# A Fourier mixer beside a gated feed-forward on one core: halved matmul groups at both ends, one product's order and one call's weights

## The chip, the cores and the metric

The kernel runs on one core of a Trainium2 chip. The metric is the device time of one launch in microseconds (us). Engines are called as the profile calls them: PE does the matmuls and PEld its weight loads, ACT and DVE work on rows of up to 128 partitions, POOL is nearly unused, and SP issues most DMAs. PSUM is the memory that PE writes, in banks of 512 fp32 columns; SBUF holds everything else on the chip.

## The reference

Input x has 2048 rows of 576 columns. After a layernorm over the columns two branches read it, and the result is the sum of x and both:

```
xn = layernorm(x)
A  = irfft2(rfft2(xn) * (w_r + i w_i))            # over rows and columns
B  = (sigmoid(xn @ w_gate) * (xn @ w_up)) @ w_down  # 576 -> 4608 -> 576
out = x + A + B
```

All of it is fp32. The kernel splits each operand of a product into a high part and a low part in PE's own format and adds three products (high x high, high x low, low x high).

## The kernel before, in words

**The feed-forward.** The 2048 rows are two pairs of 1024 rows; the columns F are 36 blocks of 128. One *unit* is one block of F for one pair: seven products of Strassen's scheme, each seven matmuls of 128x512 (`unit`, L709; `prod`, L643; `STEPS` lists the parts). The weights of a block arrive raw, ACT copies the high part (L257) and DVE subtracts the low part (L259, L261) and forms the sums that the seven products need (L281 to L284); `make_w` does this in nine pieces, and `turn(n)` advances it by n pieces at given places between the products. The down product is done per tile of 128 rows (`down`, L771): twelve matmuls of 128x288 into two PSUM banks, one for each half of the 576 columns, then one DVE add to the accumulator `acc` (L789), and for the very last block the DMA to `out` (L796): rows 0 to 63 on SP's queue, rows 64 to 127 on ACT's. The tiles still to do stand in `pend`.

**The opening.** Before the seven products can start, the first two blocks of the first pair are done plainly as four *calls* (u, c), c being the half of the 1024 rows: (0,0), (1,0), (0,1), (1,1). `opening` (L947) writes out the order by hand: moments and scales of two tiles of rows (`scaled`), `normalise` (L410, on ACT: x * rstd + nmr), transposes of the normalised tile on PE (`lift`, L430; identity weights, into PSUM), the high part on ACT (L437) and the low part on DVE (L438) into X, the transposed operand. X has five planes: two high, one remainder of 32 columns, two low. While PE has nothing to do, `identity(n)` (L929) has it multiply an identity n times. After that come the gate product and the up product of call (0,0) in `plain_late` (L691): for gate and up, and for k = 1, 2, first the six steps of `LOW_LAST` (high and low planes), then, when the remainders have been transposed (`mid`, L443 and L445), the last step. Inside `opening` most instructions go through `strictly`, which keeps program order on their engine; from the third call on `strict` is off, and the framework's scheduler orders each engine's instructions by what it expects to be ready.

**The loop over calls.** Calls three and four, (0,1) and (1,1), run `beside(i)` after each of their four products (i = 0 to 3): a down tile if there is one, then `turn(3)`. In the fourth call `make` is `make_w(2)`, the weights of the first proper unit. The same turns advance the sums and transposes for the seven products (`factors`: L418 to L425, L397, L402, L434, L443), which are in `sides`.

**The Fourier branch.** It is cut into three phases that run beside the second pair's units (`phase1b`, `phase2`, `phase3`), a piece per step (`aside`). In `phase3` (L548, 16 tiles) the inverse over the columns is this: the middle 2 x 128 frequencies and a left-over of 34 are transposed into `pz`, ACT and DVE split the former (z3h, z3l), ACT then copies the latter (z3r, L591), and a piece later come, for even and odd frequencies, one matmul of the left-over with 288 columns (L595) and six of 144 columns (L599), then ACT's copy `od` (L601).

Tile tags name PSUM: "pp" is a pair of banks with two buffers (`pair`), "bA", "bB" single banks, "bE" a bank with two buffers.

Of the kernel before, what the change touches and what calls it, by code (L numbers as in the profile page):

```python
# [13 lines left out]
OP = mybir.AluOpType  # L14
# [144 lines left out]
def spectral_glu_kernel(ctx: ExitStack, tc: tile.TileContext, x, xt, xg, ri, w_in, w_down, out):  # L159
# [11 lines left out]
    def pair(name):  # L171
        return ps.tile([P, 2, 512], F32, tag="pp", name=name, bufs=2)
# [71 lines left out]
    def strictly(ins):  # L244
        if strict[0]:
            tc.keep_in_program_order(ins)
# [163 lines left out]
    def normalise(m, c):  # L410

        t = c * TPC + m
        b, src = XS[m][:, 2 * c:2 * c + 2], acc[t].rearrange("p (a d) -> p a d", a=2)
        strictly(nc.scalar.activation(b, src, AF.Identity, bias=nmr[:, t:t + 1], scale=rstd[:, t:t + 1]))

    def sums_12(m):
        A11, A12, A21, A22, S1 = (XS[m][:, i] for i in range(5))
# [130 lines left out]
    def phase3(t):  # L548
# [43 lines left out]
        yield  # L592
        pe = pair(f"pe{t}")
        for e in range(2):
            nc.tensor.matmul(pe[:, e, :HD], zr[:3 * FR, e, :], dr[:3 * FR, e, :], start=True, stop=False, skip_group_check=True)  # L595
            for k in range(2):
                o = pe[:, e, (k + 1 + e) % 2 * HQ:((k + 1 + e) % 2 + 1) * HQ]
                for n, (l, i) in enumerate(((zh, 0), (zl, 0), (zh, 1))):
                    nc.tensor.matmul(o, l[:, k, e, :], di[:, e, k, i, :], start=False, stop=n == 2, skip_group_check=True)  # L599
        od = pool.tile([P, HD], F32, tag="od", name=f"od{t}")  # L600
        nc.scalar.activation(od, pe[:, 1, :HD], AF.Copy)  # L601
        V = pool.tile([P, 2, 2, HQ], F32, tag="ev", name=f"ev{t}")
# [37 lines left out]

    LOW_LAST = ((0, 0), (1, 1), (0, 3), (1, 4), (3, 0), (4, 1))

    def prod(bank, w, x, start, stop, skip=False, steps=STEPS):  # L643
        for j, (sx, sw) in enumerate(steps):
            strictly(nc.tensor.matmul(bank, w[:, sw, :], X[:, x, sx, :], start=start and j == 0,  # L645
                                    stop=stop and j == len(steps) - 1, skip_group_check=skip))

    def end():
# [5 lines left out]
        H[u] = (hh, hl)  # L654
        return hh, hl

    def new_plain(u, c):

        g = hp.tile([P, 2, CW], F32, tag="gv"[u % 2], name=f"g{u}_{c}", bufs=1)
        bank = [ps.tile([P, CW], F32, tag=f"b{b}", name=f"p{b}{u}_{c}", bufs=2 if b == "E" else 1) for b in ("AB"[u % 2], "E")  # L660
                if (u, c, b) != (0, 1, "A")]
        if len(bank) == 1:
            bank.insert(0, pair("pg")[:, 0])
        return g[:, 0], bank

    def gate(G_, bank):
# [9 lines left out]
    def of_plain(u, c, b, k):  # L676
        return WS[u][:, WP[f"B{k}{b + 1}"]], XA[f"A{c + 1}{k}"]
# [10 lines left out]
            beside(i)  # L688
        plain_ends(u, c, G_, bank)

    def plain_late(u, c, beside, mid):  # L691

        G_, bank = new_plain(u, c)
        beside(-1)
        for i, (b, k) in enumerate(((0, 1), (0, 2), (1, 1), (1, 2))):
            prod(bank[b], *of_plain(u, c, b, k), k == 1, False, steps=LOW_LAST)
            end()
            mid(i)
            if i < 3:
                beside(i)  # L700
        for b in range(2):
            for k in (1, 2):
                prod(bank[b], *of_plain(u, c, b, k), False, k == 2, steps=STEPS[-1:])
            if b == 0 and (u, c) != (0, 0):
                gate(G_, bank)
        beside(3)
        return G_, bank
# [63 lines left out]
    def down(p, j, m):  # L771

        t = p * TPP + m
        c, cols = m // TPC, slice((m % TPC) * P, (m % TPC + 1) * P)
        pd = pair(f"po{j}_{t}")
        for g in range(G):
            u = p * NF + j * G + g
            if (u, c) in HS:
                h, w = HS[u, c], [WF[j, g, b] for b in range(2)]
                h, w = [h[:, i, cols] for i in range(2)], [[w[b][:, i] for b in range(2)] for i in range(2)]  # L780
            else:
                h, w = [v[:, c, cols] for v in H[u]], [[WD[u][:, i, b * HD:(b + 1) * HD] for b in range(2)] for i in range(2)]
            for n, (i, k) in enumerate(((0, 0), (0, 1), (1, 0))):
                for b in range(2):
                    nc.tensor.matmul(pd[:, b, :HD], h[i], w[k][b], start=g == 0 and n == 0, stop=g == G - 1 and n == 2)  # L785

        def add():
            a = acc[t].rearrange("p (b d) -> p b d", b=2)
            nc.vector.tensor_tensor(a, a, pd[:, :, :HD], op=OP.add)  # L789
# [152 lines left out]
    def both(c, mm, mains):  # L942
        return zip(*(lift(f"A{c + 1}{h + 1}", mm, main) for h, main in enumerate(mains)))
# [3 lines left out]
    def opening():  # L947
# [48 lines left out]
        first = plain_late(0, 0, lambda i: None, mid)  # L996
        load_raw(2)
        keep_p(0)

# [213 lines left out]
    for p in range(PAIRS):  # L1213

        calls = [(0, 0), (1, 0), (0, 1), (1, 1)] if p == 0 else [(0, 0), (0, 1), (1, 0), (1, 1)]
        for n, (f, c) in enumerate(calls):
            u = p * NF + f
            if p == 0 and n == 2:
                sides += [make_d(0, 2), make_d(1, 2)]
            elif p and c == 0:  # L1220
                wd = get_d(u)
            if p == 0 and n < 2:
                if n == 0:
                    opening()
# [24 lines left out]
            if n == 3:  # L1249
                finish(make)  # L1250
# [86 lines left out]
```

## Time and profile before

| | before |
|---|---|
| median of 3 runs | 1414.44 us (1414.28 to 1415.12) |
| the profiled execution's own time | 1414.13 us |
| its span (first to last instruction) | 1412.3 us |
| PE busy | 1398.7 us, 99% of the span |
| DVE busy | 1116.6 us, 79% |
| ACT busy | 642.4 us, 45% |
| DMA | 341.48 MB, mean 242 GB/s |

How to read it: a row of the timeline gives the start in us from the span's start, the busy time, engine, line, operation, out<-in by the program's names, shape and count; neighbours of one kind are merged into one row. In brackets stands the engine's idle time before it and what ended that. A matmul's own duration overlaps the next one's, so the price of one in a stream is the distance between two starts, not its duration. The busy share is an average over stages with different limits, and has to be read stage by stage.

### The profile page before, as it was taken

Reading aid. Unit: us, or ns where it says so; the run is one execution under the profiler, and the core shown is the slowest. Engines: PE = TensorE matmul, PEld = TensorE weight load, DVE = VectorE, ACT = ScalarE, POOL = GpSimd, SP = SyncE. Lnnn points to the kernel's source line nnn. Section 1 sums busy time; section 2 is a strip of 40 time slices with the busy share of each in tenths; the row PEclk is TensorE's granted clock in tenths of the full one; section 3 lists DMA queues with packets and bytes.
Section 4 is the critical chain, followed back from the end, with each engine's and each line's share of the span. In section 5 each row is a group of like instructions: output and inputs, shape, how many; then the busy total and the mean of one; then the engine's idle time right before and its main releaser. Section 6 shows DMA issues by size and latency. Waiting matters only on the chain. (4 is left out here: it accounts for less than half of the span.)

```text
span 1412.3 us, 20690 instructions
## 1 busy us (share of the span) xinstructions
PE 1398.7 (99%) x7883; PEld 1230.3 (87%) x7883; DVE 1116.6 (79%) x1723; ACT 642.4 (45%) x1032; POOL 3.3 (0%) x5
## 2 busy tenths in 40 slices
PE   8999999999999999999999999999999999999998
PEld 6888888888888888888888888888888889888887
DVE  6998888888888888789466888867878878777884
ACT  6654444444444444443245554435545534443431
POOL 0000000000000000000000000000000000000000
PEclk9999999999999999999999999999999999999999
DMA  6588677777777776665777777678888787776643
GB/s 251 219 311 322 254 271 262 271 262 271 261 269 262 268 263 236 249 250 181 268 224 222 222 229 232 202 246 267 277 265 272 239 280 217 246 223 202 194 127 84
DMA packets 128738, 341.48 MB, mean 242 GB/s; under 512 B 11936, under 2 KB 49344, under 8 KB 123904
## 3 DMA queue, kind: packets, MB, share of 16 engines
q1 hardware_dynamic: 127712, 338.86, 70.9%
q8 instruction: 62, 1.02, 0.3%
q10 hardware_dynamic: 928, 1.31, 0.3%
q14 instruction: 36, 0.29, 0.1%
HBM read 203.99 MB, written 136.13 MB: 241 GB/s over the span
## 5 line engine op out<-in xcount | busy, mean ns | idle before, releaser
L645 PE MATMUL pB<-X,w 128*128 128x512 f32 x1484 | 380.4, 394 | 0.9 <-ACT pB L729 0.5
L645 PEld LDWEIGHTS pB<-X,w 128*128 128x128 f32 x1484 | 267.7, 188 | 51.5 <-ACT v L742 1.4
L645 PE MATMUL pE<-X,w 128*128 128x512 f32 x1064 | 272.4, 392 | 0.1
L645 PE MATMUL pA<-X,w 128*128 128x512 f32 x994 | 255.5, 392 | 0.3 <-ACT X L437 0.3
L645 PEld LDWEIGHTS pE<-X,w 128*128 128x128 f32 x1064 | 193.1, 188 | 35.6 <-DVE y L743 0.7
L785 PE MATMUL po<-wd,hh 128*128 128x288 f32 x1216 | 210.9, 295 | 0.0
L645 PEld LDWEIGHTS pA<-X,w 128*128 128x128 f32 x994 | 180.1, 188 | 32.7 <-ACT X L437 0.5
L876 PEld LDWEIGHTS ps<-wf,hs 128*128 128x128 f32 x1260 | 188.6, 188 | 20.7 <-DVE acc L886 2.0
L876 PE MATMUL ps<-wf,hs 128*128 128x288 f32 x1260 | 202.5, 296 | 0.7 <-DVE acc L886 0.4
L785 PEld LDWEIGHTS po<-wd,hh 128*128 128x128 f32 x1216 | 184.1, 188 | 11.8 <-ACT hh L768 0.4
L789 DVE TENSOR_TENSOR acc<-acc,po 128x576 f32<-128x576 f32 x168 | 125.9, 750 | 61.6 <-PE po L785 61.1
L257 ACT ACTIVATE w<-raw 128x768 fp32r<-128x768 f32 (+1 forms) x106 | 100.8, 952 | 94.8 <-PE pE L645 39.9
L785 PE MATMUL po<-wd,hl 128*128 128x288 f32 x608 | 128.7, 293 | 0.0
L886 DVE TENSOR_TENSOR qs<-qs,ps 128x576 f32<-128x576 f32 x112 | 84.1, 751 | 24.9 <-PE ps L876 24.0
L785 PEld LDWEIGHTS po<-wd,hl 128*128 128x128 f32 x608 | 98.7, 189 | 0.0
L743 DVE TENSOR_TENSOR y<-v,pE 128x512 f32<-128x512 f32 x68 | 46.7, 687 | 50.6 <-ACT v L742 49.8
L763 DVE TENSOR_TENSOR y<-y,g 128x1024 f32<-128x1024 f32 x67 | 81.9, 1223 | 3.2
L886 DVE TENSOR_TENSOR acc<-acc,ps 128x576 f32<-128x576 f32 x90 | 67.5, 751 | 21.1 <-PE ps L876 20.4
L259 DVE TENSOR_TENSOR w<-raw,w 128x512 fp32r<-128x512 f32 (+1 forms) x106 | 81.9, 773 | 2.4 <-ACT w L257 2.1
L812 ACT ACTIVATE hs<-y 128x512 fp32r<-128x512 f32 x105 | 65.0, 631 | 41.3 <-DVE y L763 14.8
L746 ACT ACTIVATE g<-pB 128x512 f32<-128x512 f32 x68 | 40.7, 599 | 88.9 <-PE pB L645 88.8
L813 DVE TENSOR_TENSOR hs<-y,hs 128x512 fp32r<-128x512 f32 x105 | 71.2, 687 | 3.9 <-ACT hs L812 3.0
(171 smaller groups left out, 1572.4 us busy)
## 6 DMA issues: line engine op xcount, KB each, us to landing
w<-wsp SPq DMA_DIRECT2D x246, 320.0 KB, 3.5
wsp<-w SPq DMA_DIRECT2D x34, 2240.0 KB, 7.8
raw<-in_w SPq DMA_DIRECT2D x34, 768.0 KB, 9.7
wdsp<-wd SPq DMA_DIRECT2D x36, 576.0 KB, 4.7
wf<-tsp SPq DMA_DIRECT2D x60, 288.0 KB, 3.5
wf<-wdsp SPq DMA_DIRECT2D x45, 288.0 KB, 3.9
std<-in_wd SPq DMA_DIRECT2D x36, 288.0 KB, 5.4
ri<-in_ri SPq DMA_DIRECT2D x16, 580.0 KB, 5.4
```

What stands on the lines that cost most here:

```text
L257: placed(nc.scalar.activation(o[:, :, :3, :], src, AF.Copy))
L259: placed(nc.vector.tensor_tensor(o[:, :, 3:, :], src[:, :, :KT, :], f32(o[:, :, :KT, :]), op=OP.subtract))
L645: strictly(nc.tensor.matmul(bank, w[:, sw, :], X[:, x, sx, :], start=start and j == 0, stop=stop and j == len(steps) - 1, skip_group_check ...
L743: nc.vector.tensor_tensor(y[:, 1], v[:, 1], bank["E"], op=OP.add)
L746: nc.scalar.activation(g[:, 1], bank["B"], AF.Sigmoid)
L763: nc.vector.tensor_tensor(y, y, g, op=OP.mult)
L785: nc.tensor.matmul(pd[:, b, :HD], h[i], w[k][b], start=g == 0 and n == 0, stop=g == G - 1 and n == 2)
L789: nc.vector.tensor_tensor(a, a, pd[:, :, :HD], op=OP.add)
L812: nc.scalar.activation(hs[:, 0], src, AF.Copy)
L813: return lambda: nc.vector.tensor_tensor(hs[:, 1], src, f32(hs[:, 0]), op=OP.subtract)
L876: nc.tensor.matmul(pd[:, i, :HD], h[:, a, m], w[:, b], start=q == 0, stop=q == 2)
L886: nc.vector.tensor_tensor(o, o, pd[:, :, :HD], op=OP.add)
```

## The change

Four edits.

1. *First gate product in column halves.* The gate product of call (0,0) is done on columns 0 to 255 of its bank as soon as the first two row tiles are in X, and on columns 256 to 511 in `plain_late` as before. The parts of the first half stand where fillers stood: two steps for each k, then three fillers where there were ten, then the transposes of tiles 2 and 3, then the four other steps. The last step (remainder) stays at full width. The bank "bA" is taken in `opening`; the transposes use the two "bE" banks first and a bank of each "pp" pair second. The normalise of tile 3 goes from ACT to DVE.
2. *Inverse over d.* In `phase3` the left-over's matmul comes behind the six others of its half, not ahead of them.
3. *Last down tile.* For the very last tile the twelve matmuls are sorted by column half, into banks "bA" and "bB"; each half has its own add, and its own store: columns 0 to 287 on SP's queue, 288 to 575 on ACT's, all 128 rows.
4. *Weights of one call later.* In the calls of the first pair the turn behind the first product (i = 0) advances `make` by no piece instead of three. Only the fourth call has something to make there.

```diff
-        strictly(nc.scalar.activation(b, src, AF.Identity, bias=nmr[:, t:t + 1], scale=rstd[:, t:t + 1]))
+        if t == 3:
+            strictly(nc.vector.tensor_scalar(b, src, rstd[:, t:t + 1], nmr[:, t:t + 1], op0=OP.mult, op1=OP.add))
+        else:
+            strictly(nc.scalar.activation(b, src, AF.Identity, bias=nmr[:, t:t + 1], scale=rstd[:, t:t + 1]))
...
         for e in range(2):
-            nc.tensor.matmul(pe[:, e, :HD], zr[:3 * FR, e, :], dr[:3 * FR, e, :], start=True, stop=False, skip_group_check=True)
             for k in range(2):
                 o = pe[:, e, (k + 1 + e) % 2 * HQ:((k + 1 + e) % 2 + 1) * HQ]
                 for n, (l, i) in enumerate(((zh, 0), (zl, 0), (zh, 1))):
-                    nc.tensor.matmul(o, l[:, k, e, :], di[:, e, k, i, :], start=False, stop=n == 2, skip_group_check=True)
+                    nc.tensor.matmul(o, l[:, k, e, :], di[:, e, k, i, :], start=k + n == 0, stop=False, skip_group_check=True)
+            nc.tensor.matmul(pe[:, e, :HD], zr[:3 * FR, e, :], dr[:3 * FR, e, :], start=False, stop=True, skip_group_check=True)
...
-    def prod(bank, w, x, start, stop, skip=False, steps=STEPS):
+    def prod(bank, w, x, start, stop, skip=False, steps=STEPS, cols=slice(0, CW)):
         for j, (sx, sw) in enumerate(steps):
-            strictly(nc.tensor.matmul(bank, w[:, sw, :], X[:, x, sx, :], start=start and j == 0,
+            strictly(nc.tensor.matmul(bank[:, cols], w[:, sw, :], X[:, x, sx, cols], start=start and j == 0,
...
+            if begun and b == 0:
+                prod(bank[b], *of_plain(u, c, b, k), False, False, True, LOW_LAST, HALF[1])
+            else:
+                prod(bank[b], *of_plain(u, c, b, k), k == 1, False, steps=LOW_LAST)
...
-        pd = pair(f"po{j}_{t}")
+        if together:
+            po = pair(f"po{j}_{t}")
+            pd = [po[:, b, :HD] for b in range(2)]
+        else:
+            pd = [ps.tile([P, CW], F32, tag=f"b{b}", name=f"po{j}_{t}_{b}", bufs=1)[:, :HD] for b in "AB"]
...
+        for b, l, r, start, stop in todo if together else sorted(todo, key=lambda v: v[0]):
+            nc.tensor.matmul(pd[b], l, r, start=start, stop=stop)
...
+            if not together:
+                for b in range(2):
+                    nc.vector.tensor_tensor(a[:, b], a[:, b], pd[b], op=OP.add)
+                    (nc.sync, nc.scalar)[b].dma_start(out[t, :, b * HD:(b + 1) * HD], a[:, b])
+                return
...
-        p1 = pair("px_A11")
-        p2 = [ps.tile([P, CW], F32, tag="bE", name=f"px_A12_{i}", bufs=2) for i in range(2)]
-        his, lows = both(0, 0, (p1[:, 0], p2[0]))
+        p1 = [ps.tile([P, CW], F32, tag="bE", name=f"px_{i}", bufs=2) for i in range(2)]
+        his, lows = both(0, 0, p1)
         for f in his:
             f()
-        identity(10)
+        bA = ps.tile([P, CW], F32, tag="bA", name="pA0_0", bufs=1)
+
+        def left(steps, first=False):
+            for k in (1, 2):
+                prod(bA, *of_plain(0, 0, 0, k), first and k == 1, False, True, steps, HALF[0])
+
         level(0, 1)
+        left(LOW_LAST[:2], True)
+        identity(3)
+        his2, lows2 = both(0, 1, [pair(f"px_A1{i + 1}")[:, 0] for i in range(2)])
         next(W[0, 2])
         for f in lows:
             f()
-        his, lows = both(0, 1, (p1[:, 1], p2[1]))
+        his, lows = his2, lows2
+        left(LOW_LAST[2:4])
+        left(LOW_LAST[4:])
         for f in his + lows:
             f()
...
-                    turn(3 if p == 0 else 1)
+                    turn(1 if p else 3 * (i > 0))
...
-        down(*pend.pop(0))()
+        down(*pend.pop(0), together=bool(pend))()
```

More of the change, by code (lines that the diff above doesn't have):

```diff
@@ L655, in new_h, with new_plain @@
         return hh, hl
-    def new_plain(u, c):
+    HALF = slice(0, CW // 2), slice(CW // 2, CW)
+    def new_plain(u, c, begun=None):
         g = hp.tile([P, 2, CW], F32, tag="gv"[u % 2], name=f"g{u}_{c}", bufs=1)
         bank = [ps.tile([P, CW], F32, tag=f"b{b}", name=f"p{b}{u}_{c}", bufs=2 if b == "E" else 1) for b in ("AB"[u % 2], "E")
-                if (u, c, b) != (0, 1, "A")]
+                if (u, c, b) not in ((0, 0, "A"), (0, 1, "A"))]
         if len(bank) == 1:
-            bank.insert(0, pair("pg")[:, 0])
+            bank.insert(0, begun or pair("pg")[:, 0])
         return g[:, 0], bank
@@ L702, in plain_late @@
             for k in (1, 2):
[L703 removed]
+                prod(bank[b], *of_plain(u, c, b, k), False, k == 2, bool(begun) and b == 0, steps=STEPS[-1:])
             if b == 0 and (u, c) != (0, 0):
@@ L784, in down @@
                 for b in range(2):
-                    nc.tensor.matmul(pd[:, b, :HD], h[i], w[k][b], start=g == 0 and n == 0, stop=g == G - 1 and n == 2)
+                    todo.append((b, h[i], w[k][b], g == 0 and n == 0, g == G - 1 and n == 2))
+        for b, l, r, start, stop in todo if together else sorted(todo, key=lambda v: v[0]):
+            nc.tensor.matmul(pd[b], l, r, start=start, stop=stop)
         def add():
             a = acc[t].rearrange("p (b d) -> p b d", b=2)
-            nc.vector.tensor_tensor(a, a, pd[:, :, :HD], op=OP.add)
+            if not together:
[3 more added lines that the diff above has]
+                return
+            nc.vector.tensor_tensor(a, a, po[:, :, :HD], op=OP.add)
             if j == NF // G - 1:
@@ L994, in mid @@
                     f()
-        first = plain_late(0, 0, lambda i: None, mid)
+        first = plain_late(0, 0, lambda i: None, mid, bA)
         load_raw(2)
```

8 lines of the change are left out of this document (4 added, 4 removed).

## The prediction

> **What bounds the kernel now.** I read the page first, for the engine that is never idle.
>
> ```profile
> span 1412.3 us, 20690 instructions
> PE 1398.7 (99%) x7883; PEld 1230.3 (87%) x7883; DVE 1116.6 (79%) x1723; ACT 642.4 (45%) x1032; POOL 3.3 (0%) x5
> ```
>
> PE is busy for 1398.7 of 1412.3 us, so an edit pays only if it takes work off PE, closes one of the few gaps in it, or shortens what lies after its last matmul. The table of windows says where the gaps can be (columns: stretch, then busy us and count of PE, PEld, DVE, ACT, POOL, then the granted clock and the DMA share).
>
> ```profile
> 40.00:50.00 10.00, 9.65 (x64) 8.69 (x62) 9.65 (x21) 7.29 (x15) 0.00 (x0) 1.00 0.50 179
> 50.00:60.00 10.00, 9.88 (x58) 8.56 (x59) 9.89 (x19) 6.32 (x13) 0.00 (x0) 1.00 0.76 289
> 60.00:100.00 40.00, 39.47 (x210) 33.41 (x208) 37.09 (x58) 21.92 (x34) 0.00 (x0) 1.00 0.78 292
> 100.00:300.00 200.00, 200.00 (x1110) 177.21 (x1109) 164.40 (x238) 91.50 (x120) 0.00 (x0) 1.00 0.77 280
> ```
>
> From 100 us on PE has no gap worth the name; a gain won earlier is carried to the end. From 40 to 60 us DVE is as full as PE (9.65 and 9.89 of 10): there the order of DVE's work decides who waits. The rest lies in the opening and behind the last matmul.
>
> **First gate product in halves, and the normalise moved to DVE.** The opening on PE, from the timeline (start, busy time, instruction):
>
> ```profile
> 10.21 2.54 PE L931 MATMUL b<-idr 128*128 128x512 f32 x10
> 12.58 1.05 PE L434 MATMUL px_A<-idf,xa 128*128 128x128 f32 x8
> 13.89 3.06 PE L645 MATMUL pA<-X,w 128*128 128x512 f32 x12 [0.25 <-ACT X L437]
> 16.78 1.52 PE L645 MATMUL pE<-X,w 128*128 128x512 f32 x6
> 18.15 0.70 PE L443 MATMUL px_r<-idr,rm 128*96 128x128 f32 x8
> 24.21 1.03 PE L434 MATMUL px_A<-idf,xa 128*128 128x128 f32 x8
> 28.00 0.44 PE L434 MATMUL px_A<-idf,xa 128*128 128x128 f32 x2 [0.24 <-ACT xa L414]
> ```
>
> The ten fillers (identity) stand from 10.21 to 12.58, 0.237 us each; the change keeps three, so 7 x 0.237 = 1.66 us of idle work goes. The twelve gate matmuls (13.89 to 16.78, 0.241 each) become 24 of 256 columns, twelve of them in the fillers' place. No 256-column matmul stands in the trace. Bounds are the nearest widths, 144 and 288:
>
> ```profile
> 1169.05 0.39 PE L599 MATMUL pe<-dit,z3h 128*128 128x144 f32 x2
> 1169.27 0.28 PE L599 MATMUL pe<-dit,z3l 128*128 128x144 f32 x1
> 1398.05 9.78 PE L785 MATMUL po<-wb,hp 128*128 128x288 f32 x72 [0.32 <-DVE acc L789]
> ```
>
> The two matmuls of 144 columns that start at 1169.05 take until the next starts at 1169.27, 0.11 each; 72 of 288 take 9.78 us, 0.136 each. I take 0.125, nearer the 288-wide row: 24 x 0.125 = 3.0 against 2.89 us, a loss of 0.1 (bounds: a gain of 0.25, a loss of 0.4). PE is left with 1.55 us less to do before 16.78. How much of it is seen depends on ACT and DVE:
>
> ```profile
> 10.05 1.09 ACT L437 ACTIVATE X<-px_A 128x512 fp32r<-128x512 f32 x2 [0.36 <-PE px_A L434]
> 11.03 1.63 ACT L414 ACTIVATE xa<-acc,nmr,rstd 128x576 f32<-128x576 f32 x2
> 13.24 1.09 ACT L437 ACTIVATE X<-px_A 128x512 fp32r<-128x512 f32 x2 [0.59 <-PE px_A L434]
> 10.60 0.68 DVE L259 TENSOR_TENSOR w<-raw,w 128x512 fp32r<-128x512 f32 x1
> 11.74 1.29 DVE L438 TENSOR_TENSOR X<-px_A,X 128x512 fp32r<-128x512 f32 x2
> 13.87 1.29 DVE L438 TENSOR_TENSOR X<-px_A,X 128x512 fp32r<-128x512 f32 x2 [0.84 <-ACT X L437]
> 16.27 0.63 DVE L402 TENSOR_TENSOR rm<-xa,rm 128x64 fp32r<-128x64 f32 x4
> 16.82 0.81 DVE L364 BATCH_NORM_STATS2 st<-acc 128x6 f32<-128x288 f32 x2
> ```
>
> Walk it. The first half products need the high parts (ACT L437, 10.65 and 11.14): they run until about 11.4, three fillers until 12.15. That wait is new; behind it on PE stand the fillers and the transposes, which could not have started before 11.9 anyway. The second transposes need both normalised tiles; ACT alone had them at 12.66, now its one is done at 11.9 and DVE's sooner, so they start near 12.2, 0.35 us earlier, and end at 13.1. Eight more halves until 14.1, the twelve of the second half until 15.6: the up product starts at 15.6 and not 16.78, 1.2 us earlier.
>
> DVE must keep up. The normalise goes in front of its L259 at 10.60. It is not on DVE in this trace; I bound it by one 288-column pass (two L364 take 0.81, so 0.41) and by DVE's 576-column add (0.75, the L789 rows below), and take 0.55. The low parts then end at 13.65 instead of 13.03, and the second pair, which before waited 0.84 us for ACT, at about 15.0 against 15.16: the added pass fits into that wait. The four L402 are then done at 16.6 to 17.0, and PE wants them (L443) at 18.15 - 1.2 = 16.95: just in time, 0.05 lost.
>
> Here a page can be weighed. The Trainium skill, VectorE: DVE Perf Modes, "Mode 2×_2P", says that a one-source fp32 operation from SBUF to SBUF streams two elements a cycle. No row here shows that; by it the pass would be near the lower bound and the 0.05 would vanish, without it near the upper and some 0.1 would be lost. Neither end changes the sum by more than 0.1.
>
> Does the lead survive the next stretch? At 24.21 PE transposes, then:
>
> ```profile
> 25.28 0.60 ACT L437 ACTIVATE X<-px_A 128x512 fp32r<-128x512 f32 x1 [2.49 <-PE px_A L434]
> ```
>
> ACT idles 2.49 us for PE; behind this copy on ACT stands the square root of the next two tiles' scales, whose normalise PE waits for at 28.00. That chain hangs on PE's own arrival, so it moves with it. **Value: -1.15 us**; bounds -0.4 (the halves at 0.136 and DVE late for L443) and -1.45 (all PE work saved).
>
> **Left-over product last in the inverse.** The same 14 matmuls in another order, 16 times.
>
> ```profile
>   ACT z3r L591: 0.5, 2
> ```
>
> This row is from the left-over product's own view (L595, idle time before it and how often): its weight load waited for ACT twice, 0.5 us in all. So that wait is 0.5 us at most. The order itself: a 288-wide matmul at the end hides the next weight load better than a 144-wide one, an estimate of a few hundredths each time from the 0.11 and 0.136 above. **Value: -0.3**; bounds -0.8 and +0.5 (0.03 us lost each time). ACT's copy (od) waits for the end of the group, which does not move.
>
> **Last down tile in halves.** The last add, the last two stores in the DMA view (KB, us from issue to landing), and an add of 288 columns from another place:
>
> ```profile
> 1407.87 0.75 DVE L789 TENSOR_TENSOR acc<-acc,po 128x576 f32<-128x576 f32 x1 [0.83 <-PE po L785]
> out<-acc SPq DMA_DIRECT2D x1, 144.0 KB, 2.4
> out<-acc ACTq DMA_DIRECT2D x1, 144.0 KB, 2.7
> L604 DVE TENSOR_TENSOR ev<-pe,od 128x288 f32<-128x288 f32 x32 | 13.1, 452 | 11.1 <-ACT od L601 11.1
> ```
>
> Sorted by half, the first six matmuls end 6 x 0.136 = 0.8 us before the last, at 1407.05; their add falls into DVE's idle 0.83 us, and its DMA leaves while PE works. Behind the last matmul stands one add of 288 columns (L604, 0.45) instead of 0.75: -0.3. Both stores wait for the one add, leave together, and the second landed 0.3 us after the first, 2.7 against 2.4; with the first gone some 0.8 us ahead, the last should land like one by itself, -0.35 or more. Its rows are 1152 bytes and twice as many, which can eat some of that. **Value: -0.7**; bounds -0.3 (the add alone) and -1.1.
>
> **Weights of one call later.** In the fourth plain call the first of four turns no longer advances the splitting of the next weights. Moved by one turn, in DVE's order: L259, L261 and L281; behind them the second and third turn's work, the store of the split weights and the load that reuses their buffer (both on SP's queue; the reloaded buffer is split one unit later, so nothing near waits for it). What the present order costs:
>
> ```profile
> 49.16 0.69 DVE L259 TENSOR_TENSOR w<-raw,w 128x512 fp32r<-128x512 f32 x1
> 49.34 0.30 PE L443 MATMUL px_S<-idr,rma 128*96 128x128 f32 x1
> 49.76 0.22 DVE L402 TENSOR_TENSOR rma<-xa,rma 128x64 fp32r<-128x64 f32 x1
> 50.12 0.24 PE L443 MATMUL px_S<-idr,rma 128*96 128x128 f32 x1 [0.48 <-ACT w L257]
> ```
>
> PE's two transposes stand 0.78 us apart because the second needs L402, which stood behind the weights' L259. With the weights later L402 goes first, and most of that gap closes. **Value: -0.5**; bounds -0.7 (this whole gap) and +6.3, the rival below. What is late next: the weights themselves.
>
> **Sum.** 1.15 + 0.3 + 0.7 + 0.5 = 2.65 us. The profiled execution took 1414.13 us, 1.8 over its span; the median of the three runs is 1414.44, 0.3 above it. So 1414.4 - 2.65 = **1411.8 us**, for the median.
>
> **Rivals.**
>
> 1. *The DVE-laden stretch pays more.* The scheduler orders everything after the opening anew, and from 60 to 100 us PE idles another 0.53 us while DVE is 93% busy. If that goes too and the tail and the inverse reach their better bounds (0.4 and 0.5 more), the sum is 4.1: 1410.3 us. For it: all these gaps end on DVE or ACT. Against it: they are small and scattered.
> 2. *The opening's lead is swallowed.* If DVE's added pass is at its upper bound and L402 makes PE wait, or the scheduler gives the lead back between 40 and 60 us where DVE is full, the opening yields 0.4 and the weights nothing: 1.4 in all, 1413.0 us. Against it: DVE waited 0.84 us for ACT just there.
> 3. *The clock.* Three fillers instead of ten leave short gaps while the clock is young. The first fillers show what a slow clock costs:
>
> ```profile
> 3.79 5.79 PE L931 MATMUL b<-idr 128*128 128x512 f32 x15 [3.79 <-DMA idr<-c_id]
> ```
>
> 15 in 5.79 us, 0.386 each, against 0.237 later. If 24 halves ran at that rate, 24 x 0.125 x 0.63 = 1.9 us would be lost: 1413.7. The Trainium skill, TensorE: Matmul & The Clock Gate, "What's actually happening", says that an idle window of about 3.4 us throttles the array; no gap in my walk is over 0.5 us, so by that rule this doesn't happen.
> 4. *Slower: the weights come too late.* DVE has 0.1 us to spare between 50 and 60 us. One turn is the distance between the weights' first two copies:
>
> ```profile
> 43.02 1.17 ACT L257 ACTIVATE w<-raw 128x1152 fp32r<-128x1152 f32 x1
> 47.10 0.85 ACT L257 ACTIVATE w<-raw 128x768 fp32r<-128x768 f32 x1 [0.84 <-DVE raw L281]
> 49.27 0.85 ACT L257 ACTIVATE w<-raw 128x768 fp32r<-128x768 f32 x1 [0.74 <-DVE raw L284]
> 51.20 0.41 DVE L261 TENSOR_TENSOR w<-raw,w 32x256 fp32r<-32x256 f32 x1
> 55.69 1.76 PE L645 MATMUL pE<-X,w 128*128 128x512 f32 x7
> ```
>
> 4.1 and 2.2 us. The last split ended at 51.61; the second product of the next unit starts at 55.69. So it decides at a delay of 4.1 us: one turn just fits, and one DVE task more does not. If this unit and the one after each wait their turn (4.1 and 2.2), 6.3 us are lost against 2.15 won elsewhere: 1418.6 us. Against it: that product needs only the second of three parts, and PE has down tiles to put in between.
>
> That an edit does nothing is nearest for the inverse, which removes 0.5 us of waits at best; it is in the range.
>
> **How the numbers follow.** Forecast 0.50, its own range 1410.8 to 1412.8; rival 1 0.25, rival 2 0.10, rival 3 0.05, rival 4 0.10. A measurement of this kernel can tell about 0.2%, 2.8 us, from no change: under 1411.6 is faster, over 1417.2 slower. The forecast stands at that edge and is split, 0.28 faster and 0.22 the same. Faster 0.28 + 0.25 = 0.53; the same 0.22 + 0.10 + 0.05 = 0.37; slower 0.10. The range takes in the forecast and rivals 1 to 3; at the low side 1 us under rival 1 for the better bounds of the opening and the weights (0.3 and 0.2) and for the scattered gaps, at the high side up to no gain at all. It leaves out rival 4: 1409.3 to 1414.4.
>
> **What would show it.** Right: the up product (pE) starting near 15.6; the second transposes near 12.2; 24 pA matmuls at 0.12 to 0.13; the transposes of 24.21 near 23.1; the two L443 at 49 us without a gap; a last add of 0.45 us and about 4.1 us from its start to the span's end; PE's waits for z3r gone. Wrong: a PE wait for DVE L402 near 17; PE waits on w in 52 to 70 us; halves at 0.2 us; a stretch after 100 us that grows.

## The result, and the profile after

| | before | after |
|---|---|---|
| median of 22 runs each, on one chip | 1414.75 us (1414.15 to 1415.59) | 1412.49 us (1411.56 to 1413.15) |
| ratio | | 0.9984, 95% interval 0.9978 to 0.9989 |
| the profiled execution's own time | 1414.13 us | 1413.03 us |
| its span | 1412.3 us | 1411.2 us |

The changed kernel is 2.26 us faster (1.6 to 3.1 by the interval). That is 0.16%, inside the bound of 0.2% that the prediction called the same. Its span fell by only 1.1 us: this one profile lost time at two places by late transfers, as told below.

The page's line of engines, then three of the windows that were shown of before (stretch, then busy us and count of PE, PEld, DVE, ACT, POOL, granted clock, DMA share, GB/s):

```profile
PE 1397.6 (99%) x7888; PEld 1229.3 (87%) x7888; DVE 1116.8 (79%) x1725; ACT 640.5 (45%) x1031; POOL 3.3 (0%) x5
```

```profile
40.00:50.00 10.00, 10.00 (x67) 9.22 (x66) 9.80 (x21) 7.08 (x14) 0.00 (x0) 1.00 0.51 179
50.00:60.00 10.00, 9.88 (x57) 8.07 (x56) 9.89 (x19) 6.61 (x13) 0.00 (x0) 1.00 0.68 256
60.00:100.00 40.00, 39.48 (x209) 33.37 (x208) 36.84 (x57) 21.38 (x33) 0.00 (x0) 1.00 0.81 308
```

PE's 0.35 us of idle time between 40 and 50 us is gone, and PE's idle time is otherwise what it was: 0.64 us between 50 and 100 us, 0.65 before.

**The opening.** The timeline of the changed kernel:

```profile
7.44 0.85 ACT L257 ACTIVATE w<-raw 128x768 fp32r<-128x768 f32 x1 [1.18 <-DMA raw<-in_w]
8.19 1.61 ACT L417 ACTIVATE xa<-acc,nmr,rstd 128x576 f32<-128x576 f32 x2
10.99 0.99 PE L648 MATMUL pA<-X,w 128*128 128x256 f32 x4 [0.26 <-ACT X L440]
11.47 0.58 DVE L415 TENSOR_SCALAR xa<-acc,rstd,nmr 128x576 f32<-128x576 f32 x1
12.51 1.04 PE L437 MATMUL px_A<-idf,xa 128*128 128x128 f32 x8
13.30 3.11 PE L648 MATMUL pA<-X,w 128*128 128x256 f32 x20
16.25 1.55 PE L648 MATMUL pE<-X,w 128*128 128x512 f32 x6
16.68 0.63 DVE L402 TENSOR_TENSOR rm<-xa,rm 128x64 fp32r<-128x64 f32 x4
17.64 0.70 PE L446 MATMUL px_r<-idr,rm 128*96 128x128 f32 x8
23.74 1.03 PE L437 MATMUL px_A<-idf,xa 128*128 128x128 f32 x8
```

The order is the one that the prediction walked through, but the lead is smaller: the up product starts at 16.25 instead of 16.78, and the transposes that stood at 24.21 stand at 23.74. The first two rows give one reason: ACT waited 1.18 us for the raw weights, and the first normalise began at 8.19. In the profile of before the same row reads

```profile
7.56 0.87 ACT L414 ACTIVATE xa<-acc,nmr,rstd 128x576 f32<-128x576 f32 x1 [0.34 <-ACT w L257]
```

so this profile of the changed kernel began 0.63 us late, by a transfer that the change does not touch. DVE was late as well. The moments of the next two tiles, which in the profile of before start at 7.38 without a wait, stood 0.90 us for their rows of the input, and that is why DVE's normalise starts only at 11.47:

```profile
8.14 0.82 DVE L364 BATCH_NORM_STATS2 st<-acc 128x6 f32<-128x288 f32 x2 [0.90 <-DMA acc<-in_x]
```

**Between 48 and 63 us.** The pair of remainder transposes that stood 0.78 us apart is one block now (48.86). Ten us later two new waits stand on PE's weight loads, both for DVE:

```profile
48.86 0.37 PE L446 MATMUL px_S<-idr,rma 128*96 128x128 f32 x2
56.82 1.85 PE L648 MATMUL pB<-X,w 128*128 128x512 f32 x7
59.22 0.12 PEld L446 LDWEIGHTS px_S<-idr,rm 128*96 128x96 f32 x1 [0.36 <-DVE rm L402]
60.19 0.42 PEld L437 LDWEIGHTS px_S<-idf,xa 128*128 128x128 f32 x4 [0.38 <-DVE X L441]
62.26 0.39 PE L648 MATMUL pB<-X,w 128*128 128x512 f32 x1
```

**At 648 us.** Counted by the matmuls of pB, the changed kernel is 0.54 us ahead of before at 616 us and level with it at 676 us. The product between, first of before, then of the changed kernel with a row from its list of DVE's waits (us in total, times, longest):

```profile
648.47 1.46 PEld L645 LDWEIGHTS pE<-X,w 128*128 128x128 f32 x7 [0.52 <-DVE y L743]
```

```profile
648.49 1.46 PEld L648 LDWEIGHTS pE<-X,w 128*128 128x128 f32 x7 [0.98 <-DVE y L751]
DVE xg L1111 <- DMA mr<-rowd: 0.5, 1, 0.5
```

DVE had waited 0.5 us for a transfer, and everything behind it on DVE came late. So this profile kept nothing of the opening's lead. The change does not touch that transfer, and the same order of instructions (x_all and x_all2 below) shows no such wait and keeps its lead there, so it belongs to this execution and not to the change. The profile of x_rest, whose opening is that of before, lost as much there by the same transfer.

**The end.** The last block's down tiles (72 matmuls in one row before):

```profile
1396.57 0.75 DVE L809 TENSOR_TENSOR acc<-acc,po 128x576 f32<-128x576 f32 x1 [0.19 <-PE po L800]
1396.90 0.69 PE L800 MATMUL po_A<-wb,hp 128*128 128x288 f32 x4
1397.42 8.14 PE L800 MATMUL po<-wb,hp 128*128 128x288 f32 x60
1405.67 0.98 PE L800 MATMUL po_B<-wb,hp 128*128 128x288 f32 x6
1406.28 0.45 DVE L806 TENSOR_TENSOR acc<-acc,po_A 128x288 f32<-128x288 f32 x1
1406.69 0.45 DVE L806 TENSOR_TENSOR acc<-acc,po_B 128x288 f32<-128x288 f32 x1
```

Before, PE waited for DVE's add at this place, [0.32 <-DVE acc L789]. Now four matmuls of the *last* tile stand there (1396.90). They can, because that tile has banks of its own and so needs no bank that an add has to release.

### The profile page after: what moved, and what is told of

The parts are those of the page before. It is cut to its first block, busy times and chain, and to the rows that moved or that the text cites. A ratio compares the mean times of both kernels' runs of the same rounds, so it can differ in the third digit from the quotient of the medians.

```text
span 1411.2 us, 20698 instructions
## 1 busy us (share of the span) xinstructions
PE 1397.6 (99%) x7888; PEld 1229.3 (87%) x7888; DVE 1116.8 (79%) x1725; ACT 640.5 (45%) x1031; POOL 3.3 (0%) x5
## 5 line engine op out<-in xcount | busy, mean ns | idle before, releaser
L648 PE MATMUL pA<-X,w 128*128 128x512 f32 (+1 forms) x1006 | 256.1, 390 | 0.4 <-ACT X L440 0.3
L259 DVE TENSOR_TENSOR w<-raw,w 128x512 fp32r<-128x512 f32 (+1 forms) x106 | 81.7, 771 | 2.4 <-ACT w L257 2.1
```

The lines of the kernel that those rows point to most:

```text
L259: placed(nc.vector.tensor_tensor(o[:, :, 3:, :], src[:, :, :KT, :], f32(o[:, :, :KT, :]), op=OP.subtract))
L648: strictly(nc.tensor.matmul(bank[:, cols], w[:, sw, :], X[:, x, sx, cols], start=start and j == 0, stop=stop and j == len(steps) - 1, skip ...
```

## The experiments

All kernels carry a switch for each edit, which shifts the line numbers by some lines; with all four on, PE, DVE and ACT have the order of the changed kernel. Every kernel was timed in 11 runs beside 33 of the kernel before, which ran on the same chip between them; the first set of four in the table below (x_all, x_halves, x_later, x_end), the second (to x_fill0) and the third have each their own 33.

| kernel | median us | ratio to before, 95% interval | difference us |
|---|---|---|---|
| x_all: all four | 1411.91 | 0.9983 (0.9974 to 0.9992) | -2.36 |
| x_halves: opening alone | 1412.70 | 0.9989 (0.9981 to 0.9998) | -1.57 |
| x_later: weights alone | 1414.32 | 1.0001 (0.9992 to 1.001) | +0.05 |
| x_end: last tile alone | 1413.57 | 0.9996 (0.9987 to 1.0005) | -0.70 |
| x_rest: inverse alone | 1414.54 | 0.9998 (0.9989 to 1.0007) | -0.40 |
| x_end_rows: all, stores by rows | 1412.73 | 0.9983 (0.9975 to 0.9992) | -2.21 |
| x_end_pair: all, last tile in a pair | 1412.50 | 0.9982 (0.9974 to 0.9991) | -2.44 |
| x_fill0: all, no fillers | 1412.46 | 0.9983 (0.9974 to 0.9992) | -2.48 |
| x_all2: all four once more | 1412.45 | 0.9981 (0.9972 to 0.999) | -2.52 |
| x_norm_act: all, normalise on ACT | 1412.92 | 0.9984 (0.9975 to 0.9993) | -2.05 |
| x_less_dve: all, less work on DVE | 1411.93 | 0.9979 (0.997 to 0.9988) | -3.04 |
| x_best: no fillers, pair | 1412.50 | 0.9982 (0.9973 to 0.9991) | -2.47 |

An interval is about 1.2 us to either side, so of the single edits only the opening is resolved by its time. The smaller terms below are read from the profiles, with the time beside them.

### One edit at a time

```diff
-HALVES, REST_LAST, SPLIT_END, LATER = True, True, True, True
+HALVES, REST_LAST, SPLIT_END, LATER = True, False, False, False   # x_halves
+HALVES, REST_LAST, SPLIT_END, LATER = False, True, False, False   # x_rest
+HALVES, REST_LAST, SPLIT_END, LATER = False, False, True, False   # x_end
+HALVES, REST_LAST, SPLIT_END, LATER = False, False, False, True   # x_later
```

A second switch (NORM_DVE) goes with the first: the normalise of tile 3 stands on DVE in x_halves and on ACT in the other three.

Expected of all four:

> All four edits once more, for a second profile. Theory A (the forecast's terms: opening 1.15, inverse 0.3, end 0.7, weights 0.5): about 2.3 to 2.6 us under before. Rival (the first profile of after taken at its word: opening 0.5, weights nothing, end 0.4, inverse 0.3, and 0.5 lost in one wait near 648 us): 0.7 to 1.1 us under before, and the wait near 648 us again 0.95 us long between two matmul starts. If the wait and the late start of the opening (normalise at 8.19 us) are chance of one execution, this profile shows neither.

Of the opening alone:

> Edit 1 alone (halves of the first gate product, three fillers, normalise of tile 3 on DVE). Theory A: 1.15 us under before, the up product (pE) 1.1 to 1.2 us earlier after the first transposes, and the lead kept to the end. Rival (the lead is 0.5 us, as the first profile has it at 21 us): 0.5 us under before.

Of the weights alone:

> Edit 4 alone (weights one turn later in the fourth call). Theory A: 0.5 us under before, kept to the end. Rival (given back at once): PE 0.5 us ahead at 57 us and level with before from 63 us on, time within 0.2 us of before. Theory of late weights: PE behind before from 55 us on.

Of the last tile alone:

> Edit 3 alone (last down tile in halves, own banks, stores by column halves). Theory A: 0.7 us under before, of which 0.3 by the shorter last add and 0.35 by a store that is not behind another; from the last matmul to the end of the span 3.8 us where before has 4.5. Rival (own banks let the scheduler put four of its matmuls into the wait for DVE's add some 10 us before the end, and the stores gain nothing): 0.5 us under before, four matmuls into po_A ahead of that wait, and still 4.5 us from the last matmul to the end.

Of the inverse alone:

> Edit 2 alone (left-over product last in the inverse). Theory A: 0.3 us under before, won in small steps between 1180 and 1390 us, because the weight load behind a 288-wide matmul is better hidden. Rival (only the two waits for z3r count): 0.1 to 0.2 us, in two steps. Nothing of it before 1168 us.

The four differences add up to -2.62 us; together they gave -2.26, -2.36 and -2.52. So the edits neither help nor hinder each other by an amount that these runs can show. The opening carries most of it; of the weights nothing can be seen. In the profile of x_all the first normalise starts at 7.44, and at 648 us it keeps its lead (0.92 us on both sides): the two losses of the changed kernel's profile were chance, as the expectation for x_all had it.

In x_halves, whose first normalise began at 7.56 as in before, the opening reads:

```profile
12.21 1.04 PE L439 MATMUL px_A<-idf,xa 128*128 128x128 f32 x8
13.00 3.11 PE L654 MATMUL pA<-X,w 128*128 128x256 f32 x20
14.17 1.73 PEld L654 LDWEIGHTS pA<-X,w 128*128 128x128 f32 x14 [0.30 <-DVE X L443]
15.95 1.55 PE L654 MATMUL pE<-X,w 128*128 128x512 f32 x6
```

The second transposes start at 12.21, as predicted (near 12.2). But the up product starts at 15.95 and not at 15.6: of these twenty, the seventh is the first that takes a low part of DVE's second pass, which ends at 14.11, and its weight load waits 0.30 us for it (14.17). Behind it the lead is not lost: the first product of call (1,0) starts at 20.22 against 21.03 in before, and the last matmul of pB at 1392.01 against 1393.14. That the lead has grown by 0.3 us is told under "Who normalises the fourth tile".

Counted from 0 as in the expectations, the 28th matmul of pB comes in x_later 36.32 us after the first (57.68 - 21.36) and in before 36.82 (57.85 - 21.03); the 35th comes after 41.76 us in both. So half a microsecond is won by 58 us and given back by 63, as that expectation's rival said. In x_end the four matmuls moved up as in the changed kernel, and the time behind the last matmul did not shrink (4.59 us, 4.48 before), both as the rival of x_end said.

### The last tile's banks and stores

```diff
-pd = [ps.tile([P, CW], F32, tag=f"b{b}", name=f"po{j}_{t}_{b}", bufs=1)[:, :HD] for b in "AB"]
+po = pair(f"po{j}_{t}")                                # x_end_pair
+pd = [po[:, b, :HD] for b in range(2)]
...
-    (nc.sync, nc.scalar)[b].dma_start(out[t, :, b * HD:(b + 1) * HD], a[:, b])
+for i in range(2):                                     # x_end_rows
+    (nc.sync, nc.scalar)[i].dma_start(out[t, i * N1:(i + 1) * N1], acc[t][i * N1:(i + 1) * N1, :])
```

> All four edits, but the last tile's halves in a pair of banks like the other tiles, not in banks of their own. Theory A (add and store shorten): no change against all four edits. Rival (own banks fill the wait for DVE): the four early matmuls are gone, 0.5 us slower than all four edits, about 1.8 us under before.

> All four edits, but the last tile's stores split by rows as before (64 rows of 2304 bytes on each queue, both behind the second add). Theory A (a store that leaves earlier and alone lands earlier): this is 0.3 to 0.4 us slower than all four edits, so about 1.9 us under before. Rival (short rows cost the store what the earlier start wins): 0.2 to 0.5 us faster than all four edits, some 2.6 us under before, and 4.1 us from the last matmul to the end.

The DMA view of the last two stores (KB each, us from issue to landing), first of the changed kernel, then of x_end_pair with its last adds and stores:

```profile
out<-acc SPq DMA_DIRECT2D x1, 144.0 KB, 3.0
out<-acc ACTq DMA_DIRECT2D x1, 144.0 KB, 3.1
```

```profile
out<-acc SPq DMA_DIRECT2D x1, 144.0 KB, 2.4
out<-acc ACTq DMA_DIRECT2D x1, 144.0 KB, 2.2
```

```profile
1396.69 9.81 PE L807 MATMUL po<-wb,hp 128*128 128x288 f32 x72 [0.31 <-DVE acc L816]
1406.55 0.82 DVE L813 TENSOR_TENSOR acc<-acc,po 128x288 f32<-128x288 f32 x2 [0.86 <-PE po L807]
```

The two versions win the same by different means. In a pair of banks the four matmuls do not move up (72 in one row again, with the wait of 0.31 in front), the last add takes 0.45 us instead of 0.75, and the stores land in 2.4 and 2.2 us: 4.09 us from the last matmul to the end, against 4.48 before. In banks of their own PE ends half a microsecond sooner, and the last stores are issued (1406.95 and 1407.18) 0.6 and 0.8 us behind those of the tile before, where x_end_pair has 1.3 and 1.7. They take 3.0 and 3.1 us, and the tail stays at 4.59. That the stores are slower because others are still under way is the likely reason, and these runs show no more than the coincidence. From the last matmul of pB to the end of the span it is 18.8 us in both (1411.24 - 1392.47 in the changed kernel, 1410.60 - 1391.77 in x_end_pair) and 19.2 before (1412.31 - 1393.14). Stores by rows gave 18.6, with 4.41 us behind the last matmul; its time (-2.21) lies between what its two theories named.

### Fillers, and a combination

```diff
-identity(3)
+identity(0)      # x_fill0; x_best: this and the pair of banks
```

> All four edits, with no fillers between the halves instead of three. Theory of the walk: the second transposes wait for the normalised tiles at about 11.9 to 12.4 us and not for PE, so at most 0.2 us changes. Rival (the clock falls back when PE rests): halves and transposes behind the gap run at twice the distance for some microseconds, 1 to 2 us slower.

> All four edits, without the three filler matmuls of the opening, and with the last tile's halves in one pair of banks, which brought the last stores home 0.4 us sooner. Theory, that the two are separate places: filler 0.1, pair 0.1 beyond all four, so 2.3 to 2.8 us less than before. Rival, that without fillers the clock is held low for longer: the up product starts later than 15.9 us and the gain is under 2 us.

```profile
12.25 1.09 PE L439 MATMUL px_A<-idf,xa 128*128 128x128 f32 x8 [0.25 <-ACT xa L419]
13.10 2.67 PE L654 MATMUL pA<-X,w 128*128 128x256 f32 x20
15.61 1.55 PE L654 MATMUL pE<-X,w 128*128 128x512 f32 x6
```

Without any filler the twenty halves still take 2.5 us from 13.10 to 15.61, 0.125 each: no slow clock follows the gap. The rival of the clock is refuted for this place. Neither kernel is faster than all four edits by an amount that can be told (-2.48, -2.47 against -2.26 to -2.52). So x_best does not beat the changed kernel, and the two gains of 0.1 that were expected of it cannot be told from none. Its up product started at 16.40, later than the 15.9 that was named as the sign of the rival; but the rival also asked for a gain under 2 us. What made the start late in this profile was the first normalise (7.86, and the second at 11.62), not a slow matmul.

### Who normalises the fourth tile

```diff
-NORM_DVE = True
+NORM_DVE = False
```

> All four edits a third time, as the reference of this set. Both theories expect 2.0 to 2.6 us less than before. In its profile the step near 1038 us (one product waits for the inverse's split) should take about 0.28 us less than in the kernel before, as it has in all kernels seen with the opening in halves and in none without.

> All four edits, but the fourth token tile is normalised by ACT as before and not by DVE. Theory: ACT then has two normalisings of 0.75 to 0.85 us one behind the other, the second four transposes wait for it, and 0.2 to 0.5 us of the opening's lead of 0.85 us at 21 us go: the time is 0.2 to 0.5 us above that of all four edits. Rival: the halves cover it, and the time stays within 0.2. Besides: if the 0.28 us at 1038 us come from ACT's having one instruction fewer ahead of that place, they are gone here, and the time is 0.3 higher once more; if they come from the matmuls of the opening, they stay.

```profile
11.43 1.63 ACT L419 ACTIVATE xa<-acc,nmr,rstd 128x576 f32<-128x576 f32 x2
13.12 0.87 PE L439 MATMUL px_A<-idf,xa 128*128 128x128 f32 x6 [0.26 <-ACT xa L419]
16.21 1.55 PE L654 MATMUL pE<-X,w 128*128 128x512 f32 x6
```

In this profile and in that of the changed kernel the second normalise starts at nearly the same time (11.43 and 11.47), and so does the up product (16.21 and 16.25). With ACT, the transposes wait 0.26 us; with DVE, the halves wait 0.3 us for the low parts behind DVE's pass. The two cancel: by this pair of profiles the rival was right about the opening. Its time is 0.47 us above that of x_all2, as the theory said though within the intervals, and what follows accounts for 0.28 of it.

The second question has a sharper answer than either theory gave. All kernels with the normalise on ACT lose some 0.3 us at one place later, but not at the same place. Before (the row of ACT's first copy behind the product `pb`) against x_all, then x_norm_act against x_all, where the numbers in brackets are ACT's idle time:

```profile
1033.79 0.65 ACT L529 ACTIVATE sw<-pb 64x580 f32<-64x580 f32 x1 [1.36 <-PE pb L527]
```

```profile
1032.54 0.65 ACT L534 ACTIVATE sw<-pb 64x580 f32<-64x580 f32 x1 [1.09 <-PE pb L532]
919.80 0.50 ACT L501 ACTIVATE ah<-pd,rstd 64x290 fp32r<-64x290 f32 x1 [1.21 <-PE pd L493]
```

```profile
920.54 0.50 ACT L501 ACTIVATE ah<-pd,rstd 64x290 fp32r<-64x290 f32 x1 [1.49 <-PE pd L493]
```

Count ACT's rows in the trace, its DMA issues and event waits included. The delayed row of before is its 960th, that of x_norm_act its 832nd; in x_all these two instructions are the 958th and the 831st, and neither is delayed. Comparing every ACT row of these kernels with the same instruction in x_all shows delays of 0.28 us in the 576th, 960th and 1088th row of before, and in the 704th and 832nd of x_norm_act. (Its 1088th starts late too, but there the profile names a transfer as what it waited for.) x_later, x_end and x_rest, which also normalise on ACT, have the same three delayed rows as before. They lie 128 rows, or a multiple, apart. Not every row of this series shows a delay: some are event waits, some follow the row before without a pause, and ACT's 576th of x_norm_act (a copy that waits 0.70 us, as it does in x_all) is not delayed, nor is the 832nd of x_all, which waits 0.58 us. So a delay of 0.28 us can fall on every 128th row of ACT, and whether it costs anything depends on which instruction happens to stand there. With all four edits ACT has two rows fewer ahead of this place than before, and the 960th is no longer a copy that PE waits for: 0.28 us of the gain is an accident of counting.

The Trainium skill, Runtime: NRT & Kernel Launch, "Instruction fetch mechanics", says that an engine's instructions are fetched in blocks of 256 and that crossing into the next block is mostly hidden. The period here is 128 rows, but a trace need not show every instruction, so it may be the same thing; no run here shows the fetch itself.

### Less work for DVE

```diff
-nc.vector.tensor_tensor(A21, A11, A21, op=OP.subtract)
 nc.vector.tensor_tensor(A12, A12, S2, op=OP.subtract)
```

> All four edits, and the four subtractions of DVE that form the third difference of the input's quarters (0.45 us each, three of them between 50 and 60 us) are left out, so that a part of the product is formed from the wrong operand; every matmul stays. Theory, that DVE's work bounds the stretch from 50 to 62 us and swallows the lead that the later weights give: the two PE waits of 0.36 and 0.38 us behind L402 and L441 at 59 and 60 us shrink to under 0.1 each, the way from the 28th to the 35th matmul of pB goes from 5.4 to about 4.9 us, and the kernel is 0.4 to 0.7 us faster than with all four edits. Rival, that the weights' transfers (DMA share 0.94 there) bound the stretch: the way stays at 5.3 us or more and the time within 0.2 us.

```profile
56.25 1.85 PE L653 MATMUL pB<-X,w 128*128 128x512 f32 x7
58.29 0.37 PE L447 MATMUL px_S<-idr,rm 128*96 128x128 f32 x2
59.78 0.42 PEld L438 LDWEIGHTS px_S<-idf,xa 128*128 128x128 f32 x4 [0.82 <-DVE X L442]
61.38 0.39 PE L653 MATMUL pB<-X,w 128*128 128x512 f32 x1
```

The kernel leaves out four subtractions of DVE. The wait for the remainder is gone (58.29, two in one block), but the wait for L441 (L442 here) grew from 0.38 to 0.82 us, where the theory asked for under 0.1. From the 28th matmul of pB at 56.25 to the 35th at 61.38 it is 5.13 us; in the changed kernel 62.26 - 56.82 = 5.44. That is between what the two theories said (4.9, and 5.3 or more), and in the direction of the first: PE won 0.3 us, and the kernel's time fell by 0.5 us against x_all2, which the intervals do not resolve. The expectation was wrong about where the work stands: of the four subtractions left out, one had stood between 50 and 60 us (58.47 in x_all2). Two others of 0.45 us that stood beside it (57.63 and 59.44) now run before 42 us, a pass of 0.75 us has moved in at 56.84, and DVE is busy for 9.86 of the 10 us, against 9.89 in x_all2. Some matmuls are ordered anew as well. So DVE's amount of work and its order changed together; that DVE bounds this stretch is supported, and this run alone does not show it.

## Why the prediction was right or wrong, point by point

**The opening (forecast -1.15).** The mechanism was right, and the size came out smaller. The start of the first product of call (1,0) scatters by almost a microsecond between profiles whose opening is the same, so it is best taken over all of them: 20.03 to 20.88 us, 20.38 on average, in the seven with edit 1 as it stands (the changed kernel, x_all, x_all2, x_halves, x_end_rows, x_end_pair, x_less_dve), and 20.92 to 21.81, 21.28 on average, in the four with the opening of before (before, x_later, x_end, x_rest). The value is 0.9 us, and this scatter leaves 1.15 within reach. The halves took 0.12 to 0.125 each, and DVE's pass 0.58 against 0.55 taken.

The step that came out otherwise is "the low parts then end at 13.65". It let DVE's normalise start at 10.60, in the place of L259. In the changed kernel and in x_halves DVE has the scales only at 11.47 and 11.17, because it had waited 0.90 and 0.36 us for the third tile's rows of the input; so the low parts of the first two tiles end past 14.1, and the half matmuls wait for them. In x_all DVE did start at 10.60, and the low parts ended at 13.54, as forecast; there the slow first fillers kept the first transposes until 9.83 (the second ones came at 12.65), and the up product started at 15.91 as well. So the walk's prices hold. What it took for granted is that the transfers and the first matmuls come when they came in the one profile of before. L402, which the prediction feared, was in time: 16.68 + 0.63 ends before 17.64. Beside that stands the 0.28 us at ACT's 960th row, which nothing in the prediction covers; with it x_halves is worth 1.1 by its profile, and 1.57 (0.3 to 2.7) by its time.

The pass took 0.58 us, in the middle between the two ends of the prediction, 0.41 and 0.75. So the rule of the Trainium skill that was weighed there (VectorE: DVE Perf Modes, "Mode 2×_2P") is not borne out in full: two adds of 288 and 576 columns, 0.45 and 0.75, give 1.04 ns for a column and 0.15 us beside; by twice the rate the pass would be 0.45, by the full price 0.75. What makes up the rest was not tried.

**The inverse (forecast -0.3).** The size was right, and it came from the order alone. From the 1100th matmul of pB to the last it is 379.60 us in x_rest and 379.83 in before, a gain of 0.23 (timed -0.40, not resolved). From 1065 us to the last matmul of pB the ten profiles with this edit gain 0.26 to 0.42 us on before, the three others without it 0.05 to 0.12. In x_rest the gain comes in steps of under 0.1 us, as its theory said and not its rival. But the sign that was named, "PE's waits for z3r gone", did not come. The wait for the left-over's copy moved to the matmuls that now stand first, and the left-over's product itself waits for nothing. From the view of L601 in the changed kernel:

```profile
  ACT z3r L594: 0.5, 2
```

**The last tile (forecast -0.7).** The profiles show 0.4 us; the timed -0.70 agrees with the forecast but is not resolved. The add of 0.45 us came. The step "the last should land like one by itself, -0.35 or more" was wrong for this version: the stores got slower, 3.0 and 3.1 us, issued close behind the others, and from the last add's start to the end it is 4.55 us, not 4.1. What came in its place, the four matmuls moved into the wait for DVE's add, the prediction had not seen, although it had quoted the row with that wait. x_end_pair shows that the forecast mechanism exists and is worth the same 0.4.

**The weights (forecast -0.5).** Wrong. The step "with the weights later L402 goes first, and most of that gap closes" happened, and PE was 0.5 us further ahead at 57.8 us than at 21. The failed step is what is late next: "the weights themselves". It was DVE, which both windows show at 9.89 of 10 us between 50 and 60 us. Work taken out of its order at 49 us was still there at 59, where the next transposes waited for it, and at 62.3 us the lead was what it had been at 21. Counted from the first product of call (1,0), DVE starts the L402 in question after 38.45 us both in before and in x_later (59.48 - 21.03 and 59.81 - 21.36): PE came to it half a microsecond earlier, and DVE no earlier at all. It is rival 2's mechanism, "the scheduler gives the lead back between 40 and 60 us where DVE is full", for the weights alone: the opening's lead passed the same stretch untouched, because everything on DVE had moved with it.

**The rivals.** Rival 1 (DVE's stretch pays more) did not happen: PE's idle time from 50 to 100 us is the same. Rival 3 (the clock) is refuted by x_fill0; its 0.386 us is moreover a mean of two paces, told in the last section. Rival 4 (weights too late, slower) did not happen: no wait of PE for w stands between 52 and 70 us.

**The sum.** Measured by the profiles: 0.9 + 0.28 + 0.23 + 0.4 + 0 = 1.8 us; x_all's span is 2.0 below that of before, and the times say 2.3 to 2.5. Where the other half microsecond lies these runs do not show; it is within the intervals. Forecast 2.65. The time of 1412.49 lies in the forecast's own range, with some luck: one term of the four was nothing, two were 0.25 and 0.3 us short, and the 0.28 us at ACT's row, which nobody forecast, made up for part of it. An estimate from these numbers puts the time without it near 1412.8, the upper end of the range. The larger chance stood on faster by over 0.2%, and 0.16% came.

## What to carry to other kernels

Where an engine is full over a stretch, moving its work within the stretch closes one wait and opens another: compare the lead of the bottleneck engine at the entrance and at the exit of the stretch, not at the wait that was removed. A wait for an add that frees a bank can be filled with matmuls that own their banks, which is worth looking for wherever an accumulator tile waits for its reader. And a difference of a few tenths of a microsecond between two programs may come from where an instruction happens to stand in its engine's stream: look for it in kernels that share the count but not the edit before it is credited to an edit.

## What the runs showed of the hardware

ACT's delay of 0.28 us, seen at rows whose numbers differ by multiples of 128, is told above.

The first matmuls run at half speed for a time that changes from run to run. Of the first fifteen fillers in x_halves the starts lie 0.43 us apart until 7.4 us and 0.23 after it; in x_all2 all fifteen are slow, the step comes only at 10.3 us or later, and there the fillers themselves hold the first transposes back (its row, then that of x_halves):

```profile
4.12 6.57 PE L957 MATMUL b<-idr 128*128 128x512 f32 x15 [4.12 <-DMA idr<-c_id]
10.53 1.03 PE L439 MATMUL px<-idf,xa 128*128 128x128 f32 x8
```

```profile
3.81 5.38 PE L957 MATMUL b<-idr 128*128 128x512 f32 x15 [3.81 <-DMA idr<-c_id]
9.02 1.10 PE L439 MATMUL px<-idf,xa 128*128 128x128 f32 x8
```

The granted clock stands at 1.00 in the windows' rows of both from 2 to 12 us, so the pace has to be read from the distance of the starts. The Trainium skill, TensorE: Matmul & The Clock Gate, "What's actually happening", says that full speed is granted after a free-running window of about 3.4 us has been busy. The step 3.6 us after the first matmul in x_halves agrees with that. The same section gives that point a spread of half a microsecond, and at another place 6, 11 or 14 slow matmuls in one kernel. Here it comes after 3.2 us and 7 matmuls in the changed kernel, and after 6.1 us and 14 or more in x_all2, which fits the second and not the first. Together with the transfers of the input and of the raw weights this makes a single profile's opening uncertain by almost a microsecond.
